# Weighted sums in bursts of four key tiles, two more turned heads, more maxima in the MLP, and PSUM banks given out by estimated reading times

## The chip, the cores and the metric

The kernel runs on one core of one Trainium2 chip. The metric is the device time of one execution in microseconds (us); before the change it is 1074.21 us, the median of three runs (1074.08 to 1075.7). The engines are TensorE (PE, matrix products into PSUM; its weight loads are PEld in the profile), VectorE (DVE), ScalarE (ACT), GpSimd (POOL) and SyncE (SP, which issues transfers).

## The reference

All arithmetic is float32. `S` is 2048 tokens, `D` 448, 16 heads of 28, one key and value head for all, `F` 1792.

```python
xn = layernorm(x)
q = (xn @ wq) as 16 heads; k = xn @ wk; v = xn @ wv
p = softmax(q @ k.T * 28 ** -0.5)
attention = (p @ v) @ wo
mlp = gelu(layernorm(xn) @ w1 + b1) @ w2 + b2
out = x + attention + mlp
```

## The kernel before, in words

The work has three stages: norms and projections, then the MLP, then the attention. The order of instructions on every engine is written out by the code; an engine runs its own list in that order.

**Products and banks.** A product of 128 columns by 512 goes into one PSUM bank ("m") that `mtile` (L114) gives out, and another engine reads it there before PE may write the bank again. In the MLP three banks go round; in the attention seven (three of `mp`, three of `mp3`, one of `mp1`), in a fixed ring (L51, L802).

**Units and steps.** The attention has 16 units, each four heads by 512 queries (`units`, L476). A unit has 16 key tiles of 128 keys and is done in eight steps of two key tiles (`steps`, L1005). For an ordinary head, a *score* (L994) makes keys by queries, with the row's maximum already folded into the product, and ACT writes its exponential to a tile "p" (L995).

**Maxima.** For that, every query's maximum is needed first: per head 16 products of queries by keys (L587), each reduced by DVE (L588). They belong to units still to come and are made early, some during the MLP and the others among the attention's steps (`max_stream`, L577; `weight`, L1009, sets how many a step gets).

**Turned heads.** In units 1 to 15, head 3 (`TURNED`, L30) goes another way. Its product has queries in the rows (L621); DVE copies it to `raw` with the scale and takes the maximum in the same instruction (L622); ACT makes the exponentials 1024 wide (L639); SP stores them to DRAM in blocks of 32 (`td`, L642), loads them back later (`load_d`, L807, tile `half`), and DVE transposes the blocks of 32 by 32 into "p" (`turn_blocks`, L975, L977). Such a head needs 16 products instead of 32.

**Weighted sums.** Four products of 32 columns each, one a head, run side by side in the array and add up `p` times values in the bank `po` (`pv`, L966). Each step ends in "P" (L1046): `BURST` = 2 key tiles of weighted sums in a row. The last unit does them in two halves of 256 queries (`pv_halves`, L949).

**A step's order** is a string of `ORDERS` (L29), one for even and one for odd steps, with or without a turned head: `s` a score with its exponential, `m` a maximum where the plan still allows one, `t` a turned score, `x` half a turned head's exponentials, `T` a block transpose, `e` the maxima of the next unit turned and loaded, `n` a piece of the division by the row sums, `o` a piece of the output projection (L842 to L844), `P` the burst. In the MLP `slot` (L714) interleaves 11 products of the first layer with 12 of the second; after every 46 / `pace` of them (L773 to L791) comes a turned score or a maximum.

## Time and profile before

| | us |
|---|---|
| median of three runs | 1074.21 |
| profiled execution, first to last instruction (its span) | 1072.6 |
| PE busy (5837 rows) | 1066.8 |
| PE weight loads busy | 716.4 |
| DVE busy (1824 rows) | 905.6 |
| ACT busy (1256 rows) | 722.7 |
| POOL busy (724 rows) | 573.9 |

The profile gives the profiled execution by its span; what lies around it up to a run's time is 1.6 us for the median. A row of the profile names line, engine, operation and tiles (written, then read), the count, the busy time and mean duration, and the idle time before it with what ended it. In the timeline a row can merge several instructions of one kind (x6), from the first one's start to the last one's end. A matrix product of 32 columns has two rows in the trace, so a burst of two key tiles (2 x 4 products) has 16. The MLP's last product starts at 459.9 us and the attention's first score at 460.1.

### The profile page before, as it was taken

The page shows a single profiled execution, that of the slowest core. Times are in us where ns is not written, and L with a number is a line of the kernel's source. Part 1 is how long each engine was busy: PE and PEld are TensorE (multiplying, and loading weights), DVE is VectorE, ACT ScalarE, POOL GpSimd, SP SyncE. Part 2 cuts the span into 40 slices and gives each one's busy share as a digit, 9 for nine tenths or more (in the row PEclk, how much of TensorE's full clock was granted, in tenths as well). Part 3 has the DMA queues.
Part 4 walks back from the last instruction along what each step waited for, and adds up shares of the span by engine and source line. Part 5 has one row for each costly group of instructions (what it writes and reads, how often), then busy time and mean ns, then how long its engine had stood idle before and what let it go on. Part 6 is the DMA issues. An engine that isn't in the chain of part 4 may idle for free.

```text
span 1072.6 us, 17598 instructions
## 1 busy us (share of the span) xinstructions
PE 1066.8 (99%) x5837; PEld 716.4 (67%) x5837; DVE 905.6 (84%) x1824; ACT 722.7 (67%) x1256; POOL 573.9 (54%) x724
## 2 busy tenths in 40 slices
PE   9999999999999999999999999999999999999998
PEld 8778888888888888865555556555556555555554
DVE  7889899988988998977998997899996999886743
ACT  6776556666667665578777775677774777765784
POOL 6679897778777888744333442433342244243120
PEclk9999999999999999999999999999999999999999
DMA  8764547677877778687888797678896778985720
GB/s 285 232 219 144 148 123 195 162 181 197 214 180 188 191 206 221 153 184 173 174 204 190 170 223 188 162 186 197 191 204 176 178 173 193 209 197 128 187 59 36
DMA packets 139368, 193.54 MB, mean 180 GB/s; under 512 B 17078, under 2 KB 95084, under 8 KB 139276
## 3 DMA queue, kind: packets, MB, share of 16 engines
q1 hardware_dynamic: 126028, 169.59, 63.0%
q0 software_dynamic: 11840, 22.25, 9.0%
q8 instruction: 46, 0.75, 0.3%
q10 hardware_dynamic: 1408, 0.57, 0.2%
q14 instruction: 46, 0.38, 0.1%
HBM read 113.38 MB, written 77.71 MB: 178 GB/s over the span
## 4 chain that ended last, share of the span: by engine, by line
PE 99%; DVE 1%; ACT 0%; issue 0%; POOL 0%; DVEq 0%; POOLq 0%
PE po L966 21%; PE m L587 19%; PE m L994 17%; PE m L704 13%; PE ph L181 10%; PE m L621 5%; PE qp L181 3%; PE ph L186 1%; PE ph L184 1%; PE m L843 1%; PE m L842 1%; PE m L844 1%; PE m L442 1%; PE po L949 1%; PE m L949 1%; PE qp L305 0%
## 5 line engine op out<-in xcount | busy, mean ns | idle before, releaser
L588 DVE TENSOR_REDUCE mx<-m 128x1 f32<-128x512 f32 x784 | 507.2, 680 | 76.2 <-PE m L587 66.1
L995 ACT ACTIVATE p<-m 128x512 f32<-128x512 f32 x784 | 402.7, 609 | 159.4 <-PE m L994 159.2
L587 PE MATMUL m<-ks,qm 128*128 128x512 f32 x784 | 321.1, 410 | 0.1
L994 PE MATMUL m<-xh,ks 128*128 128x512 f32 x784 | 257.5, 398 | 0.0
L966 PE MATMUL po<-p,vs 128*32 128x512 f32 x1920 | 230.9, 598 | 0.0
L587 PEld LDWEIGHTS m<-ks,qm 128*128 128x128 f32 x784 | 147.0, 187 | 114.1 <-ACT p L995 41.4
L622 DVE TENSOR_SCALAR_CACHE_REDUCE raw<-m 128x512 f32<-128x512 f32 x240 | 162.7, 690 | 17.3 <-PE m L621 9.1
L994 PEld LDWEIGHTS m<-xh,ks 128*128 128x128 f32 x784 | 146.2, 188 | 42.7 <-issue 5.8
L977 DVE STREAM_TRANSPOSE p<-half 128x1024 f32<-128x1024 f32 x120 | 148.2, 1236 | 5.3 <-PE m L949 2.0
L639 ACT ACTIVATE raw<-raw,m 128x1024 f32<-128x1024 f32 x120 | 133.0, 1151 | 0.0
L966 PEld LDWEIGHTS po<-p,vs 128*32 128x32 f32 x1920 | 50.1, 109 | 114.1 <-issue 109.1
L669 ACT ACTIVATE hx<-ph,b1t 128x512 f32<-128x512 f32 x55 | 37.9, 690 | 126.4 <-PE ph L186 108.6
L621 PE MATMUL m<-ks,q 128*128 128x512 f32 x240 | 93.8, 392 | 0.0
L685 POOL TENSOR_TENSOR hl<-hx,hh 128x512 fp32r<-128x512 f32 x56 | 72.5, 1294 | 29.4 <-ACT hh L683 29.4
L704 PE MATMUL m<-w2l,hh 128*128 128x448 f32 x224 | 81.0, 365 | 0.0
L704 PE MATMUL m<-w2h,hl 128*128 128x448 f32 x224 | 81.0, 366 | 0.0
L704 PE MATMUL m<-w2h,hh 128*128 128x448 f32 x224 | 80.8, 364 | 0.0
L574 POOL DMA_DIRECT2D xh<-mn x15 | 8.1, 539 | 133.1 <-ACT mn L570 133.1
L487 POOL DMA_DIRECT2D qm<-qd x120 | 61.6, 520 | 29.8 <-PE m L994 24.3
L673 POOL TENSOR_TENSOR hz<-hz,hx 128x512 f32<-128x512 f32 x56 | 72.6, 1296 | 4.6
L678 POOL TENSOR_TENSOR hx<-hx,hz 128x512 f32<-128x512 f32 x56 | 72.3, 1292 | 4.7
L181 PE MATMUL ph<-xh,w1h 128*128 128x512 f32 x165 | 65.0, 394 | 0.0
(187 smaller groups left out, 1376.6 us busy)
## 6 DMA issues: line engine op xcount, KB each, us to landing
td<-raw SPq DMA_DIRECT2D x240, 256.0 KB
half<-td SPq DMA_DIRECT2D x120, 512.0 KB
xh<-qd POOLq DMA_DIRECT2D x60, 168.0 KB, 4.3
qm<-qd POOLq DMA_DIRECT2D x120, 56.0 KB, 4.2
qd<-qe SPq DMA_DIRECT2D x24, 256.0 KB
a<-in_A_x_dram SPq DMA_DIRECT2D x24, 224.0 KB
qm<-qd SPq DMA_DIRECT2D x76, 56.0 KB
ad<-a SPq DMA_DIRECT2D x16, 224.0 KB
```

What stands on the lines that cost most here:

```text
L181: pe.matmul(ps, w, v, start=(n == 0), stop=False)
L587: pe.matmul(pm, qm[:, t * P:(t + 1) * P], ks[:, n * CW:(n + 1) * CW], start=True, stop=True)
L588: dve.tensor_reduce(mx[:, CT * j + t, n:n + 1], pm, axis=AX.X, op=ALU.max)
L621: pe.matmul(sc, q3[i][:, t * P:(t + 1) * P], ks[:, n * CW:(n + 1) * CW], start=True, stop=True)
L622: dve.tensor_scalar(raw[:, :, 4 * n:4 * n + 4, :].rearrange("p r b i -> p b r i"), sc.rearrange("p (b r i) -> p b r i", r=4, i=32), SCALE, ...
L639: act.activation(raw[:, rs], raw[:, rs], AF.Exp, bias=m3[:, 4:5], scale=1.0)
L673: pool.tensor_mul(hz, hz, hx)
L704: pe.matmul(m2[k], h[:, k * P:(k + 1) * P], w[:, ft, :], start=(ft == 0 and i == 0), stop=(ft == NF - 1 and i == 2))
L966: pe.matmul(po[32 * j:32 * j + 32, :], vs[:, kt, :], ps.pop((u, kt, j)), start=(kt == 0), stop=(kt == NT - 1))
L977: dve.transpose(p.rearrange("p k (g j) -> p g k j", j=32), halves[u, kt // 8][:, :, 32 * (kt % 8):32 * (kt % 8) + 64].rearrange("p g (k j) ...
L994: pe.matmul(s, ks[:, kt * P:(kt + 1) * P], qss[u][:, j, :], start=True, stop=True)
L995: act.activation(p, s, AF.Exp, scale=SCALE)
```

## The change

- **Bursts.** The attention goes by pairs of steps. A string of `ORDERS` is now for a pair ("|" lies between its steps); a digit stands for a burst of that many key tiles at most. Six strings serve the first pair, a unit's first pair, its others, the last steps, the last unit and the last pair. Nearly all have one burst of four.
- **Two more turned heads:** head 3 of the first unit and head 2 of the last one. The first unit's exponentials come back in two ways: a quarter (`ahead`) during the MLP's last chunk, the rest right behind the MLP. The last unit's second turned head comes back by `load_second`.
- **Maxima:** `pace` in the MLP is 21 instead of 18, so more readings for DVE lie there (310 maxima and 192 turned scores before, 390 and 192 now) and fewer in the attention.
- **Banks:** in the attention `mtile` gives out the bank that an estimate of the engines' clocks frees first (`free_at`, from the constants in `PRODUCT, LANDS, READS`), instead of the ring's next.
- **Tiles "p":** 13 pairs instead of 9, and two more in a tile that the MLP leaves free, all given out by hand in `held`.

```diff
-BURST = 2
-PAIRS = 9
-ORDERS = (("nsmsmsnomssmstmssxmP", "nsmsmsemssmsomssnxmP"), ("nmsstTmsosnmssP", "nmsmssxmeosTmsnsmP"))
-TURNED = tuple(range(1, 16))
+PAIRS = 13
+WEIGHTS = 3, 5
+ORDERS = ("nsmsmsmsonsmsmst|sxnmsmsetssnmTmT2", "nxmnnsso|snsT4mtnsemnmsssmmsosstmsT", "snmTsmsmxnsmn4|smensmmssntsmssotsoT", "sTsnesnx4s|nssssossstsnoT", "TsTTnen4sT|nsssssosno", "nTss4sTonTss|nosTsns2")
+PRODUCT, LANDS, READS = 229, 200, {"a": 480, "d": 602}
+TURNED = tuple((u, 3) for u in range(16)) + ((15, 2),)
...
+    mp = ctx.enter_context(tc.tile_pool(name="mp", bufs=1, space=PSUM))
+    banks = {"d": collections.deque(range(3))}
+    free_at, clock = {}, dict(pe=0, a=0, d=0)
...
-    def mtile(shape):
-        return next(ring).tile(shape, F32, name="m")
+    def mtile(shape, by="d"):
+        if free_at:
+            i = min(free_at, key=lambda i: free_at[i])
+            clock["pe"] = max(clock["pe"], free_at[i]) + PRODUCT
+            clock[by] = max(clock[by], clock["pe"] + LANDS) + READS[by]
+            free_at[i] = clock[by] + LANDS
+        else:
+            i = banks["d"].popleft()
+            banks["d"].append(i)
+        return (mp if i < 3 else mp4).tile(shape, F32, name=f"m{i}")
...
+        if (c, ft) == (NCH - 1, 5):
+            ahead = f(xt_p.tile([P, 4, CW], F32R, name="xh")).rearrange("p b n -> p (b n)").rearrange("p (t k) -> p t k", k=P)
+        if c == NCH - 1 and 6 <= ft < 10:
+            r = ft - 6
+            nc.sync.dma_start(ahead[32 * r:32 * r + 32], td[0, 3][:, r, :, 0:P])
+        ts, pace = 0, 21
...
-    mp3 = ctx.enter_context(tc.tile_pool(name="mp3", bufs=3, space=PSUM))
+    mp4 = ctx.enter_context(tc.tile_pool(name="mp4", bufs=1, space=PSUM))
     op = ctx.enter_context(tc.tile_pool(name="op", bufs=1, space=PSUM))
-    mp1 = ctx.enter_context(tc.tile_pool(name="mp1", bufs=1, space=PSUM))
-    ring = itertools.chain([mp] * 3 + [mp1] + [mp3] * 3, itertools.cycle([mp] * 3 + [mp3] * 3 + [mp1]))
+    free_at.update((i, k) for k, i in enumerate((0, 1, 6, 3, 2, 4, 5)))
...
-    def load_d(u, i):
-        assert stored[u] == CT - 1
+    def load_d(u, i, at=slice(0, 256)):
+        assert stored[u, 3] == CT - 1
         h, r = divmod(i, 4)
-        if r == 0:
-            halves[u, h] = att.tile([P, 4 * CT, 256], F32, name="half", bufs=3)
-        part = halves[u, h][32 * r:32 * r + 32]
-        dve.memset(part[0:1, 0, 0:1], 0.0)
-        nc.sync.dma_start(part, td[u][:, r, :, 256 * h:256 * h + 256])
+        if (u, 3, h) not in halves:
+            halves[u, 3, h] = att.tile([P, 4 * CT, 256], F32, name="half", bufs=3)
+        part = halves[u, 3, h][32 * r:32 * r + 32]
+        if u:
+            dve.memset(part[0:1, 0, 0:1], 0.0)
+        nc.sync.dma_start(part[:, :, at], td[u, 3][:, r, :, 256 * h + at.start:256 * h + at.stop])
+
+    def load_second(q, r):
+        u, j = TURNED[-1]
+        assert stored[u, j] == CT - 1
+        if q < 2:
+            if r == 0:
+                whole = keep.tile([P, 4, NT, 32], F32, name="raw", bufs=RAWS).rearrange("p r b i -> p (r b i)")
+                halves[u, j, q] = whole.rearrange("p (t k) -> p t k", k=P)
+            part = halves[u, j, q]
+        else:
+            if (u, j, 2) not in halves:
+                whole = att.tile([P, 4 * CT, 256], F32, name="half", bufs=3)
+                halves[u, j, 2], halves[u, j, 3] = whole[:, :, 0:P], whole[:, :, P:2 * P]
+            part = halves[u, j, q]
+        part = part[32 * r:32 * r + 32]
+        nc.sync.dma_start(part, td[u, j][:, r, :, P * q:P * q + P])
...
-    def turn_blocks(u, kt):
+    def turn_blocks(u, kt, j):
         p = pair_of()
+        part, k = (halves[u, j, kt // 8], kt % 8) if j == 3 else (halves[u, j, kt // 4], kt % 4)
+        if u == 0 and kt < 4:
+            part = ahead
         dve.transpose(p.rearrange("p k (g j) -> p g k j", j=32),
-                      halves[u, kt // 8][:, :, 32 * (kt % 8):32 * (kt % 8) + 64].rearrange("p g (k j) -> p g k j", j=32))
-        ps[u, kt, 3], ps[u, kt + 1, 3] = p[:, 0], p[:, 1]
+                      part[:, :, 32 * k:32 * k + 64].rearrange("p g (k j) -> p g k j", j=32))
+        ps[u, kt, j], ps[u, kt + 1, j] = p[:, 0], p[:, 1]
+        taken[id(p), 0], taken[id(p), 1] = (u, kt), (u, kt + 1)
+
+    held = [att.tile([P, 2, CW], F32, name="p", bufs=PAIRS) for _ in range(PAIRS)]
     def pair_of():
-        return att.tile([P, 2, CW], F32, name="p", bufs=PAIRS)
-
-    halfway = []
+        held.append(held.pop(0))
+        for k in range(2):
+            assert taken.pop((id(held[-1]), k), None) not in pvq
+        return held[-1]
+
+    halfway, lasts, taken = [], [], {}
...
-        s = mtile([P, CW])
+        s = mtile([P, CW], "a")
...
-    weight = [0 if n >= len(steps) - LEAD else (3, 5)[n % 2] + (u == 0) for n, (u, kt) in enumerate(steps)]
-    for n, (u, kt) in enumerate(steps):
+    weight = [0 if n >= len(steps) - LEAD else WEIGHTS[n % 2] for n, (u, kt) in enumerate(steps)]
+
+    def begin(n):
+        nonlocal loads
+        u, kt = steps[n]
         if n == 0:
             loads = pool
-        if n == len(steps) - 7:
-            ring = itertools.cycle([b for b in (next(ring) for _ in range(7)) if b is not mp1])
+        if n == len(steps) - 6:
+            free_at.pop(6)
         if n == len(steps) - 14:
             load_rows_of(NCH - 1, range(CT))
         if u + 1 < NU:
             load_d(u + 1, kt // 2)
+        if u == NU - 2 and kt >= 12:
+            for r in range(4):
+                load_second(kt // 2 - 6, r)
+        if u == NU - 1 and kt < 4:
+            for r in range(4):
+                load_second(2 + kt // 2, r)
         if 4 <= n < 4 + NG:
             prep_wo(n - 4)
         if u + 1 < NU and kt < 8:
             load_q(u + 1, (kt // 2,))
-        jobs = [(u, kt + k, j) for k in range(2) for j in range(heads_of(u))]
-        for what in ORDERS[u in TURNED][n % 2]:
-            if what == "s":
+
+    for i in range(4):
+        load_d(0, i, slice(P, 2 * P))
+    for i in range(4, 8):
+        load_d(0, i)
+    for n0 in range(0, len(steps), 2):
+        u, kt0 = steps[n0]
+        n, kt = n0, kt0
+        begin(n)
+        if n0 == 2:
+            spare = xt_p.tile([P, 4, CW], F32R, name="xh")
+            held[0:0] = [f(spare[:, k:k + 2, :]) for k in (0, 2)]
+        assert u not in mrs
+        jobs = [(u, kt + k, j) for k in range(4) for j in range(heads_of(u))]
+        turn = [(kt + k, j) for k in (0, 2) for j in (3, 2) if (u, j) in TURNED]
+        kind = 0 if n0 == 0 else 5 if n0 >= len(steps) - 2 else 4 if u == NU - 1 else 3 if n0 > len(steps) - LEAD else 1 + (kt0 > 0)
+        for what in ORDERS[kind]:
+            if what == "|":
+                n, kt = n0 + 1, kt0 + 2
+                begin(n)
+            elif what == "s":
                 score(*jobs.pop(0))
             elif what == "m":
                 if maxed < total - left + left * sum(weight[:n + 1]) / sum(weight):
                     maxed += mxs.step()
             elif what == "t":
-                tq.step()
+                if tq.step():
+                    clock["d"] += 125
             elif what == "x":
+                if exps:
+                    clock["a"] = max(clock["a"], clock["pe"]) + 1041
                 turned_exp()
             elif what == "T":
-                if u in TURNED:
-                    turn_blocks(u, kt)
+                if turn:
+                    clock["d"] = max(clock["d"], clock["pe"]) + 1165
+                    turn_blocks(u, *turn.pop(0))
             elif what == "e":
-                if kt == (6 if u + 2 < NU else 10) and u + 1 < NU:
+                if kt >= 6 and u + 1 in mrs:
                     load_max(u + 1)
             elif what == "n":
                 side.step()
             elif what == "o":
-                if n == len(steps) - 5:
-                    oside.add(o_jobs(NCH - 1, range(NG - 1)))
+                if n >= len(steps) - 5 and not lasts:
+                    lasts.append(oside.add(o_jobs(NCH - 1, range(NG - 1))))
+                worked.clear()
                 oside.step()
-            elif what == "P":
-                assert not jobs
-                for _ in range(BURST if n else 0):
-                    pv(*pvq.pop(0))
+                if worked:
+                    clock["pe"] += 2200
+                    clock["d"] += 2000
+            elif what.isdigit():
+                clock["pe"] += 320
+                for _ in range(int(what)):
+                    if pvq[0] in steps[:n] or (pvq[0][0], pvq[0][1] - 1) in steps[:n]:
+                        pv(*pvq.pop(0))
+                        clock["pe"] += 858
+        assert not jobs and not turn
```

The products on PE in a middle unit, before: two bursts (L966) and what lies between them. L587 is a maximum, L994 a score, L621 a turned score.

```order
L966 MATMUL po<-p,vs 32x512 x8
L587 MATMUL m<-ks,qm_159 128x512
L994 MATMUL m<-xh,ks 128x512 x2
L621 MATMUL m<-ks,q_161 128x512
L587 MATMUL m<-ks,qm_159 128x512
L994 MATMUL m<-xh,ks 128x512 x2
L587 MATMUL m<-ks,qm_159 128x512
L994 MATMUL m<-xh,ks 128x512 x2
L966 MATMUL po<-p,vs 32x512 x8
```

And now, the end of the stretch ahead of a burst (L999) and the start of the next one; L598 is a maximum, L1037 a score, L632 a turned score.

```order
L1037 MATMUL m_6352<-xh,ks 128x512
L632 MATMUL m_6355<-ks,q_162 128x512
L1037 MATMUL m_6359<-xh,ks 128x512
L598 MATMUL m_6368<-ks,qm_161 128x512
L1037 MATMUL m_6371<-xh,ks 128x512
L1037 MATMUL m_6374<-xh,ks 128x512
L1037 MATMUL m_6380<-xh,ks 128x512
L1037 MATMUL m_6383<-xh,ks 128x512
L999 MATMUL po<-p,vs 32x512 x16
L598 MATMUL m_6405<-ks,qm_161 128x512
L632 MATMUL m_6410<-ks,q_163 128x512
L1037 MATMUL m_6415<-xh,ks 128x512
```

Sixteen products of weighted sums stand in a row instead of eight, and 19 to 22 others between two such bursts instead of 9 or 11. Over the program there are 65 bursts instead of 127.

DVE right behind the MLP, before (L588 is a maximum, L622 a turned score):

```order
L709 TENSOR_TENSOR a<-a,m_3_4336 128x448
L813 MEMSET half 1x1
L588 TENSOR_REDUCE mx<-m 128x1 x4
L622 TENSOR_SCALAR raw,m_5360<-m 128x4x4x32
L813 MEMSET half 1x1
L588 TENSOR_REDUCE mx<-m 128x1 x6
L813 MEMSET half 1x1
L588 TENSOR_REDUCE mx<-m 128x1 x4
```

And now, some rows further on; three maxima and a turned score lie between the additions and these rows. L599 is a maximum, L1013 a block transpose, `xh` the part loaded early.

```order
L599 TENSOR_REDUCE mx<-m_5660 128x1
L599 TENSOR_REDUCE mx<-m_5666 128x1
L633 TENSOR_SCALAR raw,m_5650<-m_5672 128x4x4x32
L599 TENSOR_REDUCE mx<-m_5681 128x1
L1013 STREAM_TRANSPOSE p<-xh 128x16x2x32
L599 TENSOR_REDUCE mx<-m_5685 128x1
L1013 STREAM_TRANSPOSE p<-xh 128x16x2x32
L829 MEMSET half 1x1
L599 TENSOR_REDUCE mx<-m_5705 128x1
L1013 STREAM_TRANSPOSE xh<-half 128x16x2x32
```

Two block transposes stand in the attention's first pair of steps and a third just behind it, where there was none in the first unit.

More of the change, by code (lines that the diff above doesn't have):

```diff
@@ L1 @@
+import collections
 import itertools
@@ L56, in heads_of @@
     def heads_of(u):
-        return 3 if u in TURNED else 4
+        return 4 - sum(v == u for v, _ in TURNED)
     xv = x[0].rearrange("(p t) d -> p t d", t=NT)
@@ L1002, in o_wait @@
             yield
+        while (c, NG - 1) not in ots:
+            yield
         yield from o_jobs(c, gs, tiles)
```

34 lines of the change are left out of this document (17 added, 17 removed).

## The prediction

> **What bounds the kernel now.** First the page's head, the chain that ended last and one window (its row: stretch, then the busy time and rows of PE, weight loads, DVE, ACT, POOL, then granted clock, share of the DMA engines, GB/s).
>
> ```profile
> span 1072.6 us, 17598 instructions
> PE 1066.8 (99%) x5837; PEld 716.4 (67%) x5837; DVE 905.6 (84%) x1824; ACT 722.7 (67%) x1256; POOL 573.9 (54%) x724
> ...
> PE 99%; DVE 1%; ACT 0%; issue 0%; POOL 0%; DVEq 0%; POOLq 0%
> ...
> 701.76:737.76 36.00, 36.00 (x217) 18.49 (x216) 32.86 (x61) 27.11 (x53) 14.17 (x23) 1.00 0.79 186
> ```
>
> TensorE is busy throughout, the chain runs through it alone, and its clock is 1.00. But a busy PE can hide waits, since its ends are modelled, so I read starts in the timeline.
>
> ```profile
> 706.15 0.39 PE L587 MATMUL m<-ks,qm 128*128 128x512 f32 x1
> 706.47 1.92 PE L966 MATMUL po<-p,vs 128*32 128x512 f32 x16
> 708.32 0.50 PE L587 MATMUL m<-ks,qm 128*128 128x512 f32 x1
> 708.66 0.62 PE L994 MATMUL m<-xh,ks 128*128 128x512 f32 x2
> 709.12 0.40 PE L621 MATMUL m<-ks,q 128*128 128x512 f32 x1
> 709.35 0.39 PE L587 MATMUL m<-ks,qm 128*128 128x512 f32 x1
> 709.55 0.69 DVE L622 TENSOR_SCALAR_CACHE_REDUCE raw<-m 128x512 f32<-128x512 f32 x1
> ...
> 711.26 0.13 PEld L966 LDWEIGHTS po<-p,vs 128*32 128x32 f32 x4 [0.30 <-issue]
> 711.69 0.13 PEld L966 LDWEIGHTS po<-p,vs 128*32 128x32 f32 x4 [0.30 <-issue]
> ```
>
> Full products (128 columns by 512) start 0.23 us apart (709.12, 709.35). From the one before a burst to the second behind it are 708.66 - 706.15 = 2.51 us; less two products, a burst costs 2.05. Its 16 rows are four waves of four (one for each head; the weight loads show them), 711.69 - 711.26 = 0.43 apart, together 1.72. So 0.33 us of every burst is turning round. Check on unit 7, the window 701.76 to 737.76 (eight steps): 84 products x 0.23, 0.3 for a transpose, 8 x 2.05 = 36.0. PE waits for nothing: what is taken from PE counts in full, while VectorE (32.86 of 36.00 busy) and the PSUM banks keep up.
>
> **The change, part by part.** Prices of the readers:
>
> ```profile
> L995 ACT ACTIVATE p<-m 128x512 f32<-128x512 f32 x784 | 402.7, 609 | 159.4 <-PE m L994 159.2
> L966 PE MATMUL po<-p,vs 128*32 128x512 f32 x1920 | 230.9, 598 | 0.0
> ...
> 700.01 3.04 ACT L995 ACTIVATE p<-m 128x512 f32<-128x512 f32 x6 [0.53 <-PE m L994]
> ...
> 701.10 1.24 DVE L977 STREAM_TRANSPOSE p<-half 128x1024 f32<-128x1024 f32 x1
> ...
> 702.26 1.25 DVE L588 TENSOR_REDUCE mx<-m 128x1 f32<-128x512 f32 x2
> ...
> 704.15 1.89 DVE L588 TENSOR_REDUCE mx<-m 128x1 f32<-128x512 f32 x3 [0.52 <-PE m L587]
> ...
> 76.17 2.47 DVE L588 TENSOR_REDUCE mx<-m 128x1 f32<-128x512 f32 x4
> ...
> 76.89 0.19 PEld L587 LDWEIGHTS m<-ks,qm 128*128 128x128 f32 x1 [0.41 <-DVE mx L588]
> ```
>
> A maximum takes (1.89 - 0.69) / 2 = 0.60 us where several run in a row, a turned score 0.69 (its row at 709.55), a block transpose 702.26 - 701.10 = 1.16, an exponential (3.04 - 0.61) / 5 = 0.49. A product is readable 709.55 - 709.12 = 0.43 after it starts, and its bank comes back 76.89 - 76.17 = 0.72 after a maximum starts to read it.
>
> *Bursts.* 1920 rows by 16 are 120 bursts, and 7 in the last unit; the new order has 65. The waves stay. 62 x 0.33 = **20.5 us less**.
>
> *Two turned heads.* Each drops 16 maxima and 16 scores on PE and adds 16 turned scores: 2 x 16 x 0.23 = **7.4 us less**. VectorE gets 32 x (0.69 - 0.60) + 16 x 1.16 + 8 small reductions x 0.16, some 22.7 us more; ACT gains 16 wide exponentials and loses 32 narrow ones, which is next to nothing. VectorE's share is hidden beside PE as long as the waits below stay small; without that cover it would cost up to its 22.7 us.
>
> Without waits that is 1072.6 - 27.9 = 1044.7. Now what is late next.
>
> *More maxima in the MLP.* By the order, the MLP's readings for DVE go from 502 to 582. For PE the move is free, since these products only change their place; the question is VectorE in the MLP (rows of 100 to 400 us, then the last chunk's additions):
>
> ```profile
> L588 DVE TENSOR_REDUCE mx<-m 128x1 f32<-128x512 f32 x225 | 149.6, 689 | 10.0 <-PE m L587 2.9
> L622 DVE TENSOR_SCALAR_CACHE_REDUCE raw<-m 128x512 f32<-128x512 f32 x156 | 105.1, 690 | 13.8 <-PE m L621 7.3 <-DMA td<-raw 1.8 <-PE ph L181 0.8
> ...
> 458.93 2.20 DVE L709 TENSOR_TENSOR a<-a,m 128x448 f32<-128x448 f32 x4
> ```
>
> From 100 to 400 us it makes 381 readings, one per 0.79 us, mean 0.64 and about 0.04 for the rest: 86%. With 61 more (and 61 x 0.23 us) there is one per 0.71: 95%. PE comes back to the same of the three banks after 2.1 us, and a bank's trip (product, reading, return) takes 0.43 + 0.72, so VectorE may be 0.95 us behind before PE waits. Four additions at a chunk's end (2.20 us, while PE's own twelve products and five maxima take 3.6) overrun that by some 0.6, at four chunk ends. Bounds: 0, and 80 x (0.60 - 0.23) = 30 if VectorE were full. It isn't by these rows: **2 us**.
>
> *The first unit's turned head.* Its transposes come right behind the MLP, and stand in DVE's order ahead of maxima, so a late transfer holds those, and through them the banks.
>
> ```profile
> 459.56 1.91 SPq L710 DMA_DIRECT2D ad<-a  x4
> 460.11 0.40 PE L994 MATMUL m<-xh,ks 128*128 128x512 f32 x1
> ...
> 462.02 1.69 SPq L821 DMA_DIRECT2D wor<-in_A_wo_dram  x4
> ...
> 460.00:475.00 15.00, 15.00 (x77) 8.22 (x76) 11.18 (x25) 12.15 (x25) 7.96 (x10) 1.00 1.02 225
> ```
>
> DVE is through the additions at 461.1. In the new order 8 maxima, 2 turned scores and 2 transposes (of the part loaded early) stand before the third transpose: wanted at 461.1 + 8.5 = 469.6. Its four transfers (1 MB) are issued at 463.7 behind 1.7 MB of `ad` and `wor`; at the 225 GB/s that these DMA engines reach when full (share 1.02) they land at 460 + 2.7 / 0.225 = 472. The next 2 MB land at 481, wanted about 480. The first burst also waits for the first transpose (467.2), where PE, from 460.1 on with 21 products, would be at 465. So 2 + 2 + 1, partly over each other; bounds 0 and 7: **4 us**.
>
> *Banks in the long bursts.* A burst now takes 3.43 + 0.33 us in which no product is made, and all products crowd into the 4.4 to 5 us between. I walked three windows of unit 7 product by product: a product starts 0.23 after the last and not before its bank is back (0.72 after a maximum starts; after an exponential I take its 0.61 and 0.05 more). In the window with 12 scores, 8 maxima and 2 turned scores, PE waits 0.26 us, most at the product behind the last turned score, where the bank of the sixth, a score, comes back at 3.79 against 3.59; in the one with 6 maxima 0.1; in the one with 5 none. A unit's four windows lose 0.46; units 1 to 10 have this shape: **5 us**. Bounds: 0, and 60 x 0.26 = 16.
>
> *VectorE over a unit:* 25 maxima, 8 turned scores, 8 transposes and 1.4 for small ones are 31.2 us, of 81 x 0.23 + 0.3 + 4 x 3.76 = 33.9 (92%; before 91%). So it is no fuller than before on the average; what changes is that it must live through 3.76 us on what it has in hand. The new table puts a transpose just ahead of each burst and another a few steps before it, and at the start of a burst one or two transposes and two or three maxima wait, 2.4 to 4.1 us of work. I take nothing for it beyond the banks' 5 us; what it costs if that cover is thin is the third rival.
>
> *The rest.* The last unit's second turned head adds 8 transposes and 4 MB of transfers; a window there has 8 scores, 1.8 + 3.76 us, against four transposes, 4.6. Burst and transposes are a pair apart, which hides 4 us of lateness; 0, at most 4. SP's 32 more stores ride where the DMA engines stand at 0.79.
>
> Sum: 1044.7 + 2 + 4 + 5 = 1055.7 against the profiled span; the median before is 1.6 above its span (1074.2, 1072.6), so **1057**.
>
> **Rivals.** *No new wait* (the planner's table removes them; for it: PE waits for no bank today): 1044.7 + 1.6 = 1046. *Banks dear*: every window pays like the heaviest, 16 instead of 5: 1068; for it, most banks in my walk come back within 0.03 us of use.
>
> *Slower: VectorE becomes the bound.* Place: just behind each burst, where it already waits 0.52 us for PE (the row at 704.15). If its stock runs out in the burst of 3.76 us, its 31.2 us a unit are cut up by idle stretches that nothing gives back, and the unit is 31.2 plus four of them. At 1.5 us of idle time that is 37.2 instead of 33.9; 14 units lose 46, and 1044.7 + 2 + 4 + 46 + 1.6 = 1098. It turns slower than before where the units lose 22 in all, 1.6 each, which is 1.1 us of idle time per burst. Against it: the stock of 2.4 to 4.1 us at a burst's start, and only some 0.77 us (0.34 to the second product, 0.43 until it is readable) until the next maximum.
>
> [...]
>
> *The change does nothing*: turning round is hidden by something that the trace doesn't show, and its removal only moves a wait; 1074. The closing sum for unit 7 speaks against it.
>
> **How the numbers follow.** Forecast 0.58, no new wait 0.16, banks dear 0.14, nothing 0.03, VectorE bound 0.09. Faster by over 0.2% (about what a measurement here can tell): 0.88; same 0.03; slower 0.09. The range runs from the no-wait case, 1046, to just past the dear banks, 1070, and leaves the last two out.
>
> **What would show it.** 65 bursts, most of 32 rows, with 2.51 + 1.72 = 4.2 us from the product before to the second behind. If right, DVE stays below 96% in the MLP, PE's start-to-start excess is near 5 us in units 1 to 10, and PE shows gaps of some us shortly after the MLP. It would be wrong if DVE's idle time behind bursts reached 1.1 us, if waits for transposes showed in many units, or if MLP slots grew past the added products.

## The result and the profile after

The changed kernel takes 1077.3 us (median of 17 runs, 1076.4 to 1079.5) where the kernel before takes 1074.2: a ratio of 1.0031, with a 95% interval of 1.0023 to 1.0038. It is slower by 3 us; 1057 was forecast, and 1070 was the end of the range. First the head of its page and the shares of the chain of work that ended last, then unit 7 as one window (columns as in the prediction).

```profile
span 1075.8 us, 17796 instructions
PE 1058.8 (98%) x5805; PEld 714.2 (66%) x5805; DVE 914.1 (85%) x1880; ACT 723.9 (67%) x1240; POOL 563.2 (52%) x704
...
PE 93%; DMA 2%; DVE 2%; ACT 2%; issue 1%; SPq 0%; POOL 0%; ACTq 0%; DVEq 0%; POOLq 0%
...
749.48:784.61 35.13, 35.13 (x218) 17.84 (x210) 30.99 (x63) 29.27 (x55) 12.09 (x19) 1.00 0.96 221
```

TensorE is busy for 8 us less (1066.8 before), and still the end is 3.2 us later. The chain was 99% TensorE; now 7% of it lies on transfers, VectorE, ScalarE and issue. So time was taken off TensorE and came back as waits. The unit's window shows why a busy column can't tell this: TensorE counts as busy for all of its 35.13 us, though the sum of the prediction has 33.9 us of work in it.

Where the time lies, by the starts of certain products in the two traces (a unit's length runs from the last row of the unit before to the last row of its own weighted sums):

| stretch | before | changed | changed, by the sum without waits |
|---|---|---|---|
| start to the MLP's last product | 459.9 | 480.6 | 478.3 |
| unit 0 | 44.5 | 45.0 | 35.5 |
| unit 1 | 36.0 | 39.7 | 33.9 |
| units 2, 3, 4, 6, 7, 8, each | 36.0 | 35.1 | 33.9 |
| units 10, 11, 12, each | 36.0 to 35.0 | 33.1 to 33.6 | 31.9 to 32.1 |
| from unit 14's last row to the end | 42.2 | 40.3 | not worked out |

(80 moved products are 18.4 us for the MLP; unit 0 has 86 products, 32 waves of 0.43 and five turnings; units 10 to 12 have no turned scores left.) The sum without waits was 1044.7, the span is 1075.8: 31 us were lost. The MLP has 2.3 of them, units 0 and 1 have 14 (9.5, and 5.8 less some 1.2 that unit 1 loses like those behind it), and some 15 are spread over the units from 1 on, 1.1 to 1.5 in each but units 5, 9 and 13. These have 48 output products besides (9.7 us: 45.7 of unit 5 in the kernel before, less 36.0); they take 43.7, 44.1 and 41.8 us, and by counts of their own products they lose just 0.3, 0.5 and nothing.

**What a wait for a bank looks like.** TensorE, its weight loads and ScalarE in the timeline, in the first crowded window of unit 7. In brackets stand the idle time and what ended it.

```profile
750.00 0.50 PE L598 MATMUL m<-ks,qm 128*128 128x512 f32 x1
750.34 0.40 PE L632 MATMUL m<-ks,q 128*128 128x512 f32 x1
...
751.02 5.21 ACT L1038 ACTIVATE p<-m 128x512 f32<-128x512 f32 x10 [0.23 <-PE m L1037]
...
752.36 0.32 PEld L1037 LDWEIGHTS m<-xh,ks 128*128 128x128 f32 x2 [0.19 <-ACT p L1038]
...
753.43 0.90 PE L1037 MATMUL m<-xh,ks 128*128 128x512 f32 x2
753.83 0.19 PEld L1037 LDWEIGHTS m<-xh,ks 128*128 128x128 f32 x1 [0.30 <-ACT p L1038]
753.94 0.19 PEld L598 LDWEIGHTS m<-ks,qm 128*128 128x128 f32 x1
...
754.17 0.40 PE L598 MATMUL m<-ks,qm 128*128 128x512 f32 x1
...
755.38 0.42 PE L1037 MATMUL m<-xh,ks 128*128 128x512 f32 x1
...
755.73 3.64 PE L999 MATMUL po<-p,vs 128*32 128x512 f32 x32
...
759.30 0.50 PE L1037 MATMUL m<-xh,ks 128*128 128x512 f32 x1
...
759.64 0.39 PE L598 MATMUL m<-ks,qm 128*128 128x512 f32 x1
```

The weight load at 753.83 waited for an exponential's bank; it starts with its product, where the load at 753.94 starts 0.23 ahead of its own (754.17), and that product starts 0.40 us after the last one (753.43 to 753.83, the row of two), 0.17 late. The next, at 754.17, waited for nothing and is still 0.34 behind: 0.11 more, as its load started 0.11 behind the one that waited. So this wait cost 0.11 on top. In the second window a product is on time, and its wait cost as much:

```profile
761.60 0.39 PE L598 MATMUL m<-ks,qm 128*128 128x512 f32 x1
761.82 0.30 PEld L1037 LDWEIGHTS m<-xh,ks 128*128 128x128 f32 x2 [0.25 <-ACT p L1038]
761.83 0.73 PE L1037 MATMUL m<-xh,ks 128*128 128x512 f32 x2
...
762.40 0.41 PE L632 MATMUL m<-ks,q 128*128 128x512 f32 x1
```

The first of the two scores starts 0.23 behind the maximum, but its load just 0.01 ahead of it; from there to the second product behind are 0.57 us instead of 0.46. Unit 7 has five such places, and in each the product behind starts 0.33 to 0.34 us later, whether the one that waited was 0.17 late or on time. In the first window, from 750.00 to 755.38, lie 22 products: 5.38 - 0.34 - 20 x 0.23 = 0.44 us lost. The same for the unit's four windows, beside my walk: 0.44 (0.26 forecast), 0.34 (0.1), 0.16 (0.1), 0.16 (0). That is 1.1 us, and 1.2 with the transposing product in the second one, for which 0.11 has to be added; the kernel before loses within 0.03 in each of its windows.

The burst itself came as forecast: 759.64 - 755.38 = 4.26 us from the product before to the second behind (4.2 forecast; the median of 59 bursts is 4.26).

**The start of the attention.** The third transpose, as a late transfer held it, and three stretches of ten microseconds:

```profile
498.13 1.25 DVE L1013 STREAM_TRANSPOSE xh<-half 128x1024 f32<-128x1024 f32 x1 [5.93 <-DMA half<-td]
499.30 0.65 DVE L599 TENSOR_REDUCE mx<-m 128x1 f32<-128x512 f32 x1
500.01 0.30 PEld L1037 LDWEIGHTS m<-xh,ks 128*128 128x128 f32 x2 [4.71 <-DVE mx L599]
500.01 0.73 PE L1037 MATMUL m<-xh,ks 128*128 128x512 f32 x2 [4.28 <-DVE mx L599]
...
501.44 0.63 PE L1037 MATMUL m<-xh,ks 128*128 128x512 f32 x1
...
501.86 0.63 PE L598 MATMUL m<-ks,qm 128*128 128x512 f32 x1
...
504.36 0.40 PE L598 MATMUL m<-ks,qm 128*128 128x512 f32 x1
...
530.69 0.69 DVE L633 TENSOR_SCALAR_CACHE_REDUCE raw<-m 128x512 f32<-128x512 f32 x1 [3.35 <-DMA td<-raw]
...
531.45 0.70 PE L598 MATMUL m<-ks,qm 128*128 128x512 f32 x1 [2.99 <-DVE raw L633]
```

```profile
490.00:500.00 10.00, 5.73 (x30) 2.34 (x28) 3.14 (x5) 3.29 (x7) 0.55 (x1) 1.00 1.13 210
500.00:510.00 10.00, 9.88 (x51) 5.48 (x52) 7.97 (x18) 7.51 (x14) 4.99 (x10) 0.83 1.13 224
...
530.00:540.00 10.00, 8.55 (x46) 4.63 (x47) 8.09 (x15) 5.15 (x9) 1.88 (x4) 0.83 1.06 189
```

The transfer held VectorE for 5.9 us, VectorE the banks, and the banks TensorE for 4.3. Behind that gap the granted clock is 0.83 in the mean of ten microseconds, and products start 0.42 us apart (501.44, 501.86) and take 0.63; at 504.36 one takes 0.40 again. At 530 it happens again for another reason: a turned score finds its buffer still on its way out (`td` from `raw`), TensorE stands for 3 us, and the clock is 0.83 once more. The DMA engines are full in these stretches (1.13, 1.13, 1.06).

So behind a gap of 4.28 us products are 0.42 apart from 501.44 on, and 0.23 apart again from 504.36 on (504.36, 504.59, 504.82). Behind the gap at 531.45, 2.99 us by its row and 3.38 from start to start (528.07 to 531.45), they are 0.42 to 0.43 apart from 531.95 to 534.93 and 0.23 from 535.42 on.

### The profile page after: what moved, and what is told of

Same layout as the page of the kernel before. It is cut to its first block, busy times and chain, and to the rows that moved or that the text cites. A ratio compares the mean times of both kernels' runs of the same rounds, so it can differ in the third digit from the quotient of the medians.

```text
span 1075.8 us, 17796 instructions
## 1 busy us (share of the span) xinstructions
PE 1058.8 (98%) x5805; PEld 714.2 (66%) x5805; DVE 914.1 (85%) x1880; ACT 723.9 (67%) x1240; POOL 563.2 (52%) x704
## 4 chain that ended last, share of the span: by engine, by line
PE 93%; DMA 2%; DVE 2%; ACT 2%; issue 1%; SPq 0%; POOL 0%; ACTq 0%; DVEq 0%; POOLq 0%
PE po L999 19%; PE m L1037 17%; PE m L598 16%; PE m L715 12%; PE ph L192 11%; PE m L632 6%; PE qp L192 3%; PE ph L195 1%; PE m L874 1%; PE ph L197 1%; PE m L876 1%; PE m L875 1%; DMA half<-td 1%; DMA td<-raw 1%; ACT p L1038 1%; PE po L982 1%
## 5 line engine op out<-in xcount | busy, mean ns | idle before, releaser
L599 DVE TENSOR_REDUCE mx<-m 128x1 f32<-128x512 f32 x752 | 484.7, 682 | 73.7 <-PE m L598 69.7
L1038 ACT ACTIVATE p<-m 128x512 f32<-128x512 f32 x652 | 342.4, 623 | 112.2 <-PE m L1037 109.4
L598 PE MATMUL m<-ks,qm 128*128 128x512 f32 x752 | 289.4, 400 | 4.1 <-DVE raw L633 3.0
L1037 PE MATMUL m<-xh,ks 128*128 128x512 f32 x752 | 261.4, 416 | 4.8 <-DVE mx L599 4.3
L999 PE MATMUL po<-p,vs 128*32 128x512 f32 x1664 | 219.5, 595 | 0.9 <-DVE p L1013 0.9
L1037 PEld LDWEIGHTS m<-xh,ks 128*128 128x128 f32 x752 | 139.1, 189 | 100.9 <-issue 40.8
L633 DVE TENSOR_SCALAR_CACHE_REDUCE raw<-m 128x512 f32<-128x512 f32 x272 | 181.7, 687 | 12.7 <-PE m L632 6.1
L598 PEld LDWEIGHTS m<-ks,qm 128*128 128x128 f32 x752 | 141.9, 189 | 43.8 <-issue 11.7
L650 ACT ACTIVATE raw<-raw,m 128x1024 f32<-128x1024 f32 x136 | 153.0, 1163 | 0.0
L1013 DVE STREAM_TRANSPOSE p<-half 128x1024 f32<-128x1024 f32 x112 | 137.8, 1234 | 1.5 <-DMA half<-td 1.1
L999 PEld LDWEIGHTS po<-p,vs 128*32 128x32 f32 x1664 | 55.0, 109 | 108.7 <-issue 105.3
L632 PE MATMUL m<-ks,q 128*128 128x512 f32 x272 | 108.1, 398 | 0.1
L1038 ACT ACTIVATE xh<-m 128x512 f32<-128x512 f32 x100 | 55.9, 624 | 21.5 <-PE m L1037 21.0
L999 PE MATMUL po<-xh,vs 128*32 128x512 f32 x256 | 64.7, 595 | 0.0
```

Of the source, the lines that this page charges most:

```text
L598: pe.matmul(pm, qm[:, t * P:(t + 1) * P], ks[:, n * CW:(n + 1) * CW], start=True, stop=True)
L599: dve.tensor_reduce(mx[:, CT * j + t, n:n + 1], pm, axis=AX.X, op=ALU.max)
L632: pe.matmul(sc, q3[i % 2][:, t * P:(t + 1) * P], ks[:, n * CW:(n + 1) * CW], start=True, stop=True)
L633: dve.tensor_scalar(raw[:, :, 4 * n:4 * n + 4, :].rearrange("p r b i -> p b r i"), sc.rearrange("p (b r i) -> p b r i", r=4, i=32), SCALE, ...
L650: act.activation(raw[:, rs], raw[:, rs], AF.Exp, bias=m3[:, 4:5], scale=1.0)
L999: pe.matmul(po[32 * j:32 * j + 32, :], vs[:, kt, :], ps.pop((u, kt, j)), start=(kt == 0), stop=(kt == NT - 1))
```

## The experiments

My theory from the two traces was: the turning round is saved as forecast, and given back by (a) the transfers at the start, (b) products that wait for banks in the crowded windows between long bursts, (c) the MLP. The rivals: that products are further apart for a reason of TensorE's own; that VectorE's order is at fault; that at the start the order of the transfers decides and not their volume.

### The first unit without its turned head

```diff
-TURNED = tuple((u, 3) for u in range(16)) + ((15, 2),)
+TURNED = tuple((u, 3) for u in range(1, 16)) + ((15, 2),)
...
+        if u == 0:
+            kind = 6 + (n0 > 0)
```

(with strings of 16 scores for unit 0, and without `ahead` and its loads)

> The changed kernel with its first unit's head 3 computed directly again (16 scores more and 16 turned scores fewer; no transfers of a turned head behind the MLP). Theory (the start of the attention is lost to the transfers' volume: the DMA engines are full from 490 to 540 us, and TensorE waits for transposes and for VectorE): the 14 us come back, 3.7 us of products are added; from the MLP's last product to the end of unit 1 some 75 us instead of 84.7, time 1067. Rival (the start is slow for something else: the crowd of products behind the first bursts, or the clock by itself): the products are only added, 1081.

Measured: 1086.4 us, ratio 1.0111 (1.0096 to 1.0127). Units 0 and 1 took 77.3 us (75 were expected), but units 2 to 7 took 36.7 to 38.9 (here and below without unit 5, which has output products too). My strings had put only five turned scores into unit 0 where the others have eight; from then on turned scores met buffers that were not yet stored (three such waits on VectorE from 600 to 670 us, 5.8 together). That came with my edit, so the total (1067 expected) says nothing of the start. Once more with eight:

> The first unit's head 3 computed directly again, as in the run before that did so, but with eight turned scores in the first unit as in the others (that run had five; VectorE's turned scores and ScalarE's wide exponentials got out of step, and units 2 to 7 took 38 us). Theory (the start of the attention is lost to transfers): units 0 and 1 together 77 us instead of 84.7, as in that run, and units 2 to 8 at 35.1; time 1070. Rival (the loss only moves to later units, because VectorE or the transfers have to catch up anyway): units 2 to 8 above 36, time 1077 or more.

Measured: 1072.5 us, ratio 0.9986 (0.9977 to 0.9996). Units 0 and 1 take 77.4 where the changed kernel takes 84.7, the units behind 35.4 (each has one product more, 0.23). With this head computed directly, the whole is 4.8 us faster: the head saves 3.7 us of products and costs 11 in waits.

### Order or volume

```diff
-    for j in range(4):
-        src = wo.rearrange("(g j d) n -> j d g n", j=4, d=DH)[j]
-        nc.sync.dma_start(wor[32 * j + 1:32 * j + 1 + DH, :, :], src)
...
     for i in range(4, 8):
         load_d(0, i)
+    for j in range(4):
+        src = wo.rearrange("(g j d) n -> j d g n", j=4, d=DH)[j]
+        nc.sync.dma_start(wor[32 * j + 1:32 * j + 1 + DH, :, :], src)
```

> The changed kernel with the four loads of the output weights moved behind the first unit's twelve loads of its turned head, so that these land sooner by what 0.8 MB take, some 3.6 us. Theory (the DMA engines are full from 490 to 540 us and the volume decides): the waits move within the start, units 0 and 1 together stay at 84.7 within 1.5, time 1077. Rival (the order of the transfers decides, as I reckoned it at first: the third transpose's wait of 5.9 us shrinks by 3.6 and the rest follows): 81, time 1073.5.

Measured: 1076.7 us, ratio 1.0025 (1.0015 to 1.0036); units 0 and 1 together 84.6. The wait moved, from the head's transposes to the output weights, which ScalarE must split in its order:

```profile
ACT woh L853 <- DMA wor<-in_A_wo_dram: 9.5, 1, 9.5
...
PE m L598 <- ACT p L1035: 6.0, 1, 6.0
```

(the list of waits from 480 to 562 us: sum, times, longest). So this change of order wins nothing. The other side, the volume alone, on top of unit0_plain_2:

```diff
+    for i in range(8):
+        h, r = divmod(i, 4)
+        if r == 0:
+            idle = att.tile([P, 4 * CT, 256], F32, name="half", bufs=3)
+        at = slice(P, 2 * P) if h == 0 else slice(0, 256)
+        nc.sync.dma_start(idle[32 * r:32 * r + 32, :, at], td[1, 3][:, r, :, 256 * h + at.start:256 * h + at.stop])
```

> unit0_plain_2 with twelve loads (3 MB) put where the changed kernel loads the first unit's turned head, of the same shapes, into two tiles that nobody reads: the volume without a transpose that waits for it. Theory (volume: full DMA engines make the other transfers late too, stores of turned scores and the next unit's halves among them): units 0 and 1 together go from 77.4 to 82 or more, time 1077. Rival (the loss is the waiting transposes alone, with the banks that they hold up): 77.4 within 1, time 1072.5.

Measured: 1084.0 us, ratio 1.0090 (1.0075 to 1.0105). Units 0 and 1 take 88.8: loads that nobody reads (3 MB, in eight transfers and not in twelve) cost 11.4 us, as much as the head's 11. The timeline shows where, and the windows the engines around it, of this run first and then of unit0_plain_2:

```profile
520.88 20.37 SPq L825 DMA_DIRECT2D half<-td  x4
...
535.07 0.69 DVE L633 TENSOR_SCALAR_CACHE_REDUCE raw<-m 128x512 f32<-128x512 f32 x1 [10.53 <-DMA td<-raw]
535.82 0.80 PE L598 MATMUL m<-ks,qm 128*128 128x512 f32 x1 [10.15 <-DVE raw L633]
```

```profile
500.00:510.00 10.00, 9.79 (x56) 4.88 (x55) 5.48 (x13) 9.25 (x19) 3.29 (x4) 1.00 1.12 220
510.00:520.00 10.00, 10.00 (x61) 5.33 (x64) 5.40 (x15) 10.00 (x20) 3.67 (x5) 1.00 1.12 214
...
530.00:540.00 10.00, 4.18 (x12) 3.37 (x13) 4.73 (x10) 2.46 (x5) 0.00 (x0) 0.56 0.97 204
```

```profile
500.00:510.00 10.00, 9.79 (x57) 4.99 (x56) 5.41 (x14) 9.27 (x18) 3.27 (x4) 1.00 0.84 171
510.00:520.00 10.00, 10.00 (x62) 5.14 (x65) 5.41 (x15) 10.00 (x21) 3.88 (x5) 1.00 0.71 163
```

Without the loads the DMA engines stand at 0.84 and 0.71, with them at 1.12. TensorE goes on until 525, some 30 us behind the issue of the last of them (the changed kernel, which has its loads at the same place, issues them from 484.5 to 496.4); then a store of turned scores is late, VectorE stands for 10.5 us, TensorE for 10.2, and the clock is 0.56. So the volume is enough for the whole loss, and in the two orders of loads that were tried the order only chose which transfer is waited for. Whether the stores would fare better ahead of the loads or on another engine's queue wasn't tried.

### Bursts of two in the changed kernel

```diff
-"nxmnnsso|snsT4mtnsemnmsssmmsosstmsT", "snmTsmsmxnsmn4|smensmmssntsmssotsoT"
+"nx2mnnsso|snsTmtnsemns2msssmmosstmsT", "sn2mTsmsmxnsmn|smensm2mssntsmssotsoT"
```

(and so in the strings of the last units)

> The changed kernel with each burst of four split into two of two, half a window apart; all else as changed. Theory (in the long bursts' crowded windows products wait for banks, 1.2 us a unit, and at two by two they don't): units 2 to 12 pay 4 x 0.33 more for turning round and lose no more time to banks, 35.2 us where they took 35.1; time 1077, within 3. Rival (products are 15 ns further apart for a reason that has nothing to do with the bursts' length): the units pay 1.3 us more each, 36.4; time 1094.

Measured: 1223.8 us, ratio 1.1392, units at 46.7. With the first pair's burst in place, each burst took the two key tiles whose transposes had been issued just ahead of it, and waited for VectorE. That tells nothing of banks. With the bursts a step further behind:

> The changed kernel with each burst of four split into two of two, and the first pair's burst dropped, so that each burst is a step further behind its transposes than in the run before (there bursts waited for transposes placed just ahead of them). Theory (products wait for banks in the crowded windows of the long bursts only): the excess per product goes, 4 x 0.33 us of turning round come back, units 2 to 8 at 35.0; time 1077, within 3. Rival (products are further apart for another reason): 36.4 a unit, 1094.

Measured: 1091.5 us, ratio 1.0158 (1.0143 to 1.0173): by the total a miss, in four of the units that it was made for a hit. Units 3, 4, 6 and 8 take 35.2 to 35.3; the windows of units 7 and 8 lose at most 0.03 us each, but for one wait of 0.6 in unit 7. Units 2 and 7 have such a wait (36.05), and unit 14 takes 36.2 instead of 29.9, with a transpose that waits 7.7 us for the last unit's loads, which my order doesn't fit; units 0 and 1 take 2.9 more together. So with bursts of two the waits in the other windows are gone, and the 1.3 us of turning round that return are all that long bursts had been worth: 35.25 against 35.1. Long bursts gain 0.1 to 0.2 us in such a unit, not 1.3. In units 5, 9 and 13 they gain 1.0, 0.6 and 1.3 (44.7, 44.7 and 43.1 us with bursts of two). There 48 output products with only four readings lie between the bursts; that they are why the saving stays is likely, but not tested.

### Long bursts alone in the kernel before

```diff
-BURST = 2
-PAIRS = 9
+BURST = 4
+PAIRS = 13
...
-                for _ in range(BURST if n else 0):
+                for _ in range(0 if n % 2 == 0 else BURST if n > 1 else 2):
```

> The kernel before with bursts of four only (every second step, 13 pairs of tiles; its ring, its orders, its heads and its MLP stay; the output additions wait for their last group in the order). Theory (long bursts save 4 x 0.33 us a unit in turning round and give at least as much back to waits for banks, as the crowd of products between them is denser here than in the changed kernel: 28 us of VectorE's work and the ring): units 2 to 4 between 35.8 and 36.8 instead of 36.0, time 1070 to 1085. Rival (the saving stands by itself, and the changed kernel loses it elsewhere): units at 34.7, time 1056.

Measured: 1140.6 us, ratio 1.0619 (1.0603 to 1.0635). Units 2 to 4 take 41.2 to 41.6. The direction was right, the size far off. The window of unit 3, and the waits that are in it:

```profile
593.26:634.81 41.55, 37.78 (x220) 18.56 (x213) 32.90 (x61) 27.66 (x53) 14.21 (x23) 1.00 0.69 162
```

```profile
ACT p L997 <- PE m L996: 13.5, 7, 3.8
DVE mx L588 <- PE m L587: 8.1, 4, 2.6
```

VectorE does the same 32.9 us as before the change, and waits 8.1 us in four places, 2 us behind each burst: 41. This is my third rival, VectorE as the bound, and it is true of long bursts on the old ring and the old order. The four windows of this unit lose 1.3, 1.5, 1.6 and 1.6 us to banks. (The edit brings one wait of its own, 0.8 us a unit: a burst now lies across the units' boundary and waits in its middle until ScalarE has emptied `po`.) The same row of the changed kernel's unit 7:

```profile
DVE mx L599 <- PE m L598: 3.5, 4, 1.0
```

There VectorE waits 0.9 us behind each burst, just short of the 1.1 from which I had reckoned that this rival decides. So the rest of the change, the planner, the order and the maxima in the MLP, lets the changed kernel bear long bursts. Of these the planner is worth 6 us to the changed kernel (below); the order and the maxima weren't tried apart.

### The MLP's part alone

```diff
-        ts, pace = 0, 18
+        ts, pace = 0, 21
```

(in the kernel before)

> The kernel before with the MLP's pace of readings at 21 instead of 18, so with some 80 maxima more in the MLP and as many fewer in its attention, and nothing else. Theory (the MLP pays 0.03 us per moved reading over TensorE's 0.23, and the old attention waits for nothing, so it gives back just the products): the MLP's last product 20.7 us later, the attention 18.4 us shorter, time 1076.5. Rival (the old attention has waits for VectorE that its 80 fewer maxima take away): 1072 or less. Rival (the MLP's loss comes with other parts of the change): 1074.

Measured: 1076.6 us, ratio 1.0027 (1.0017 to 1.0036). The MLP's last product starts at 480.56, as in the changed kernel; 2.3 us are lost and nothing is gained elsewhere.

### Transposes under the burst

```diff
-"nxmnnsso|snsT4mtnsemnmsssmmsosstmsT", "snmTsmsmxnsmn4|smensmmssntsmssotsoT"
+"nxmnnssoTT|sns4mtnsemnsmsssmmosstms", "snmsmsmxnsmTTn4|smensmmssntsmssotso"
```

> The changed kernel with both block transposes of a pair of steps put right ahead of its burst of four, so that VectorE does them while TensorE makes no product; nothing is added or left out. Theory (VectorE's 1.17 us of a transpose in the crowded windows holds the banks): the 15 ns of excess per product fall by half or more, units 2 to 8 take 34.4 instead of 35.1, time 1069. Rival (the excess isn't VectorE's, but comes with exponentials or from TensorE itself): units stay at 35.1, 1077. Rival (VectorE lags anyway and now has its transposes late): units above 35.1, over 1077.

Measured: 1076.9 us, ratio 1.0028 (1.0018 to 1.0037); units at 35.2, as against 35.1. So where VectorE does its transposes made no difference here. This theory of the waits fell.

### Shorter readings, not told and told

```diff
-                    dve.tensor_reduce(mx[:, CT * j + t, n:n + 1], pm, axis=AX.X, op=ALU.max)
+                    dve.tensor_reduce(mx[:, CT * j + t, n:n + 1], pm[:, 0:CW // 2], axis=AX.X, op=ALU.max)
```

> The changed kernel with each maximum taken over the first 256 of its 512 columns, so that it reads for some 0.27 us less (half of the keys are left out of the maxima). Theory (banks that VectorE returns late are what spaces the products): the excess of 15 ns per product nearly goes, units 2 to 8 take 34.1 instead of 35.1, and the MLP's 2.3 us go; time 1063. Rival (exponentials hold the banks, or TensorE itself): units stay within 0.3 of 35.1; time 1073 or more.

Measured: 1074.6 us, ratio 1.0005 (0.9996 to 1.0014). The MLP's last product is 2.6 us earlier; units 2 to 8 stay at 35.1, though a maximum takes 418 ns in the mean instead of 682, and VectorE has 25.2 us to do in a unit instead of 31.0. I had expected 34.1. The same kernel once more, with the planner's times as they were:

> As half_max, once more under this name only if the planner's constant is the same; see the next run.

Measured: 1074.8 us, ratio 1.0005 (0.9995 to 1.0014), units at 35.1 again. Then with the planner told:

```diff
-            clock[by] = max(clock[by], clock["pe"] + LANDS) + READS[by]
+            short = 267 if by == "m" else 0
+            by = "d" if by == "m" else by
+            clock[by] = max(clock[by], clock["pe"] + LANDS) + READS[by] - short
...
-                    pm = mtile([P, CW])
+                    pm = mtile([P, CW], "m")
```

> Maxima over the first 256 of 512 columns, as in half_max (half of the keys are left out of the maxima), and the planner is told that a maximum reads 267 ns less. In half_max units 2 to 8 stayed at 35.1, but there the planner still gave out banks by the old times, so a bank that came back early went unused. Theory (the excess is the wait for banks as the planner gives them out): now units 2 to 8 take 34.5; with the MLP's 2.2 and the first unit as in half_max, time 1068. Rival (VectorE's readings play no part in the excess): units stay at 35.1, time 1074.7 as for half_max.

Measured: 1066.1 us, ratio 0.9925 (0.9908 to 0.9941). Unit 7 of half_max and of this run as windows, and the waits of scores' weight loads for exponentials in that unit (sum, times, longest), half_max first; in this run the lines stand two further on:

```profile
747.49:782.60 35.11, 35.11 (x218) 17.68 (x210) 25.23 (x62) 29.18 (x54) 12.05 (x19) 1.00 0.99 223
```

```profile
742.06:776.40 34.34, 34.34 (x217) 18.53 (x210) 25.14 (x62) 29.18 (x55) 12.72 (x20) 1.00 1.00 229
```

```profile
PEld m L1037 <- ACT p L1038: 3.1, 15, 0.3
```

```profile
PEld m L1039 <- ACT p L1040: 0.3, 1, 0.3
```

The same work on every engine, 0.8 us apart (0.9 in the mean of six units, 34.2 against 35.1). What differs is which bank a product is given. As long as the plan is fixed by the old times, banks that VectorE returns early lie idle and TensorE waits for those that ScalarE reads. So the excess is waits for banks, shown from both sides, and TensorE's own spacing is ruled out but for the 0.3 us by which 34.2 is still above the 33.9 of the sum.

### The ring in the planner's place

```diff
-            free_at[i] = clock[by] + LANDS
+            free_at[i] = max(free_at.values()) + 1
```

> The changed kernel with banks given out in a fixed ring of seven instead of by estimated reading times; all else as changed. Theory (in the crowded windows a product waits for the bank that it was given; walked with the measured durations, the ring makes 36.0 a unit where the planner makes 35.1 to 35.3): units 2 to 8 at 36.0, time 1085. Rival (the order in which banks are given out is worth nothing, as I counted it at first): 35.1 a unit, 1077.

Measured: 1083.5 us, ratio 1.0083 (1.0068 to 1.0098); units 2 to 8 at 35.3 to 35.6, the profiled span 1079.4. The planner is worth 0.25 us in most of these units, 0.8 to 1.1 in units 5, 9 and 13, and 6 us by the medians (3.6 by the profiled executions); less than walked, and not the nothing that I took.

### Scores and maxima in turn

```diff
-"nxmnnsso|snsT4mtnsemnmsssmmsosstmsT", "snmTsmsmxnsmn4|smensmmssntsmssotsoT"
+"nsxnnosT|ns4nsmsmsmsenmssstmosmTstm", "nsmTxsmnnms4|smensmsmssntmssmosostT"
```

(on unit0_plain_2)

> unit0_plain_2 with the two strings of the middle units written so that a score comes first behind a burst and scores and readings for VectorE alternate in the crowded stretch; the same operations, transposes and digits. Theory (a bank is waited for where three or four scores stand in a row and ScalarE, at 0.49 us each, falls behind TensorE's 0.23): walked with the measured durations, a unit loses 0.7 us less: units 2 to 7 at 34.7 instead of 35.4, time 1064. Rival (the excess doesn't come from the order of the readers): 35.4 a unit, 1072.

Measured: 1070.4 us, ratio 0.9966 (0.9954 to 0.9978). Units 2 to 7 take 35.3 to 35.75, not 34.7; unit 8, which has no turned scores in these two runs, 33.4 instead of 34.15, and units 11 and 12 0.3 less. So the walk's gain came only where there are no turned scores. Of the versions here that compute everything, this one and unit0_plain_2 are faster than both kernels, by 0.3% and 0.1% of the kernel before. Which order would take the waits away in the other units stays open.

## Why the prediction was wrong

- **Bursts, -20.5: right.** 4.26 us were measured from the product before to the second behind, 4.2 forecast.
- **Two turned heads, -7.4: right for the products**: TensorE has 5805 rows where it had 5837. VectorE's longer work (914.1 for 905.6) sets no end by itself.
- **MLP, +2: right**, 2.3; alone in the kernel before it is the same.
- **"The first unit's turned head": 4 us, bounds 0 and 7; it cost 11 to 14.** This step failed. It took two due times of the first transposes and the transfers ahead of them, and counted lateness as something that passes. Its first due time was already 5 us off (below). And in that stretch 3 MB more fill the DMA engines (1.12, where they stand at 0.84 and 0.71 without them) and make others late, past the transposes and into the stores of turned scores 30 us on: plain_and_3mb, where transposes wait for just 0.6 us, lost 11.4 us to it. Each gap of 3 to 4 us also brought a stretch of products 0.42 to 0.43 us apart instead of 0.23, some 1.7 us by the starts, which I hadn't counted.
- **"Banks in the long bursts": 5 us; it cost some 15.** This step was sized wrong, its mechanism right. The walk's 0.26, 0.1 and 0 a window were 0.44, 0.16 to 0.34 and 0.16. It counted a wait of 0.03 us as 0.03 and left out that the product behind a waited one is 0.1 late as well; unit 7 has five of these, 0.5 of the 0.7 us that were missing from its sum. And it counted units 1 to 10, where units 11, 12 and 14 lose 1.1 to 1.5 us each too. The rival "banks dear" came near with its 16, in part by luck: the windows don't pay alike (0.16 to 0.44), and more units pay than it counted.
- **"Rest 0"**, the planner among it: the planner is worth 6 us to the changed kernel (ring), so without it the change would have lost more.
- **The rival on VectorE** was right about its place and didn't decide here: behind a burst VectorE waits 0.9 us in the changed kernel. That VectorE isn't the bound there is shown by half_max: with 5.8 us less for it to do, a unit takes 35.1 as before. In before_burst4, with 2 us, it decides.

The due time that was 5 us off: the third transpose's transfers were to be there 12.4 us behind the first row of `ad`, after 2.7 MB. In the changed kernel that row stands at 480.35, and the transpose started at 498.13, 17.8 us behind. These are the stretches from 480.35 to the forecast due time and to the transpose:

```profile
480.35:492.70 12.35, 10.98 (x51) 5.74 (x53) 10.35 (x20) 7.52 (x15) 5.83 (x6) 1.00 0.96 227
480.35:498.13 17.78, 14.01 (x69) 6.88 (x67) 10.35 (x20) 9.38 (x19) 6.38 (x7) 1.00 1.01 221
```

12.35 us at 227 GB/s are 2.8 MB, so the rate was right. But 3.9 MB (17.78 at 221) had moved before the transpose could start: some 1.2 MB that the term put behind these transfers, or nowhere, went along with them.

1057 plus 10 for the start and 10 for the banks is 1077.

So the changed kernel is slower not since its parts do nothing: long bursts alone cost 66 us, and the planner, the new order and the maxima moved to the MLP together bring them back to about even. Leaving out the first unit's turned head alone gives 4.8 us back.

## What to carry to other kernels

A stall that is removed on the bounding engine may not count in full if the buffers behind it have no slack: here long bursts save 1.3 us a unit in turning round, and 1.1 of it went into waits for banks in unit 7. So walk the crowded stretch with what a wait costs in the trace, its after-effect too (0.11 us here), and not with the length of the wait. Extra transfers that fill the DMA engines can cost nearly the time that they take to move: here 3 MB at the 214 GB/s of a full stretch, 14 us, cost 11.4, and putting others behind them won nothing. And a plan of buffers that is fixed ahead by estimated times can lose what the estimates miss: here shorter readings (418 ns for 682) left a unit at 35.1 us, and at 34.2 once the plan knew of them.

## What the runs showed of the hardware

- In unit 7 of the changed kernel a product whose weight load waited for a bank, and started with the product or 0.01 us ahead of it, was up to 0.17 us late, and the next one started 0.33 to 0.34 instead of 0.23 us behind it, though it waited for nothing (five places). The rows at 753.83 and 753.94 are one of them: the load that waited starts with its product, the next one 0.23 ahead of its own.
- Behind gaps of 3.0, 4.3 and 10.2 us the granted clock was 0.83, 0.83 and 0.56 in a window of ten microseconds, and products were 0.42 to 0.43 us apart for some 3 us.
- 3 MB of loads without a reader took 11.4 us from a kernel whose DMA engines stood at 0.84 and 0.71 in two stretches there; with the loads they stood at 1.12 in both, and the time was lost at 525 to 536 us, some 40 us after the loads began (484.5 in the changed kernel, which has its loads at the same place).
